# When the weight copies of a seven-product stage are stored, and how fast its weight sums are formed: a sliding-window attention and mixer kernel on one core

## The chip, the cores and the metric

The kernel runs on one core of one Trainium2 chip. The metric is device time in microseconds (us) of one execution; lower is better. The kernel before takes 866.21 us, the median of three runs (866.21, 866.83 and 866.21). One further execution was profiled: it took 867.31 us, and its span from the first to the last instruction is 865.5 us.

The core has five instruction queues that run side by side and meet only through semaphores: TensorE (PE, whose weight loads are listed apart as PEld), VectorE (DVE), ScalarE (ACT), GpSimd (POOL) and SyncE (SP). In this kernel SP issues nearly all DMA transfers, in the order of its queue. Each queue is worked through in order: an instruction that waits holds up all that stand behind it on its engine.

## The reference, cut to what matters

Eight batches of 576 tokens, eight heads of 64. Attention looks back over a window of 64 positions; its result, laid out as `x` with 576 rows of 512 per batch, goes through a token mixer and a channel mixer.

```python
scores = where((rel >= 0) & (rel < 64), q @ k.T / 8, -1e9)
x = softmax(scores) @ v                                   # per batch: 576 x 512
h = maximum(x.T @ w_tok1, 0) @ w_tok2                     # 512 x 576, over the tokens
u = x + h.T
h2 = maximum(u @ w_ch1, 0) @ w_ch2                        # 512 -> 1536 -> 512
out = u + h2
```

The four weight matrices arrive as 64-bit floats. Everything below happens in the last two lines: the channel mixer with `w_ch1` (512 x 1536) and `w_ch2` (1536 x 512).

## The kernel before

**Precision.** An fp32 matrix is held as two parts, `hi` (its rounding to the type float32r) and `lo` (the rest), and a product is three matmuls: hi by hi, hi by lo, lo by hi. Writing a part pair takes one ACT instruction (`hi`, a copy or a Relu) and one DVE instruction (`lo`, a subtraction).

**The two stages.** The first stage works over 36 tiles of attention and the token mixer and leaves `u` in DRAM (`u_dram`). The second stage is the channel mixer. It takes the 8 * 576 = 4608 tokens in nine chunks of 512. For one chunk, the *first product* makes twelve row blocks (`ft` = 0 to 11, 128 of the 1536 hidden rows each): `gemm1` is 12 matmuls (4 blocks of the 512 input rows times 3) into one PSUM bank `gp`, then `relu_split` writes `ghi` on ACT (line 607) and `glo` on DVE (line 608). The *second product* makes four output blocks (`ct` = 0 to 3): `gemm2` runs over the hidden blocks into a bank `op`, `add_out` adds the bank to `uf` on DVE (line 633) and, when the output block is complete, SP stores it (line 635).

**Chunks 0 to 2 are plain.** Chunk 0 runs all twelve `gemm1`, then four `gemm2` of 36 matmuls each. Chunks 1 and 2 run in two halves: six `gemm1` (72 matmuls), then four `gemm2` of 18 matmuls (72 matmuls), then the same for the other six blocks. In the first half of chunk 1, `load_u` fetches chunk 2's `u`; in the second half, behind `ft` = 8, `split_u` splits it into parts (four ACT and four DVE instructions).

**Chunks 3 to 8 go in pairs.** For a pair of chunks the first product is done as a 2 x 2 x 2 block product with seven products instead of eight (`PRODUCTS`: m1, m6, m7, m5, m2, m4, m3; line 839). Its weights are seven combinations of four quarters of `w_ch1`. Three of them (m1, m2, m4) are quarters as they are; four (m5, m7, m6, m3) are sums and differences. All seven, in both parts, must lie in DRAM (`w1s`) in the order in which they will be read: from chunk 2 on, `load_w1` reads them back in pieces, over the place in SBUF that held the plain weights `w1hi` and `w1lo`.

**Who makes `w1s`.** The generator `weight_steps` does it during chunk 1. Its first call issues twelve stores from SP, 384 KB each: m1, m2 and m4, two column blocks each, two parts each, straight from `w1hi` and `w1lo`. Then follow sixteen steps, four for each of n = 0 to 3 (a quarter of the work: 384 columns of one column block). With n fixed, the four steps are:

- A: two DVE additions (hi + lo) make `wa` and `ws`.
- B: two DVE additions, then `keep("m5")`.
- C: two DVE subtractions, then `keep("m7")` and `keep("m6")`.
- D: one DVE addition, one DVE subtraction, then `keep("m3")`.

A `keep` is a split (one ACT cast `whi`, one DVE subtraction `wlo`) and two stores of 192 KB from SP. The tiles `whi` and `wlo` have four buffers each, so a `keep` must wait until the two stores of the `keep` four before it have landed.

**What sets the order.** The order of each engine's queue is the order in which the code is written; there is no scheduler. In chunk 1 each `gemm1` with its `relu_split` is followed by two calls of the generator (lines 768 to 770). The generator's instructions so stand in the ACT and DVE queues between one block's `ghi` and `glo` and the next block's.

Of the kernel before, what the change touches and what calls it, by code (L numbers as in the profile page):

```python
# [10 lines left out]
F32 = mybir.dt.float32  # L11
# [11 lines left out]
P = 128  # L23
# [7 lines left out]
NCT = C // P  # L31
# [52 lines left out]
def mixer_kernel(ctx: ExitStack, tc: tile.TileContext, qh, kh, vh, wt1, wt2, wc1, wc2, out):  # L84
# [464 lines left out]
    with ExitStack() as bctx:  # L549
# [91 lines left out]
            return ps.tile([P, CHUNK], F32, name=f"op{name}_{ct}", tag=tag, bufs=bufs)  # L641


        u = ul.pop(0)
        for ft in range(NFT):
            gemm1(0, ft, u, gbuf[ft])
# [10 lines left out]
        for ct in range(NCT):  # L657
            for _ in range(7):
                next(late, None)
            assert all(n in finished for n in range(23 + 4 * ct, 27 + 4 * ct))  # L660
            op = new_op("0", ct)
            gemm2(op, ct, range(NFT), gbuf, True, True)
            add_out(0, u[0], ct, op, True)
        tctx.close()


        pw = tctx.enter_context(tc.tile_pool(name="pw", bufs=1, reuse_waits="tile"))

        def store_w1(m, k, f0, ct, src):

            nf = src.shape[1] // P
            nc.sync.dma_start(w1s[k][:, f0:f0 + nf, PRODUCTS.index(m), ct],  # L672
                              src.bitcast(F32).rearrange("p (f c) -> p f c", c=P))

        def weight_steps():
            for m, half, ct0 in (("m1", 0, 0), ("m2", 0, 2), ("m4", 1, 2)):
                for ct in range(2):
                    for k, w in enumerate((w1hi, w1lo)):
                        o = (half * NCT + ct0 + ct) * NH * P
                        store_w1(m, k, 0, ct, w[:, o:o + NH * P])  # L680
            yield
            nf = CW // P
            for n in range(2 * NH // nf):
                ct, f0 = n % 2, n // 2 * nf

                def whole(tag, half, ct):
                    o = (half * NCT + ct) * NH * P + f0 * P
                    t = pw.tile([P, CW], F32, name=f"{tag}_{n}", tag=tag, bufs=1)
                    nc.vector.tensor_add(t, w1hi[:, o:o + CW].bitcast(F32), w1lo[:, o:o + CW].bitcast(F32))
                    return t  # L690

                def keep(m, x):
                    hi, lo = (pw.tile([P, CW], F32R, name=f"w{k}_{m}_{n}", tag=f"w{k}", bufs=4) for k in ("hi", "lo"))
                    split(nc.scalar, nc.vector, hi, lo, x)
                    for k, t in enumerate((hi, lo)):
                        store_w1(m, k, f0, ct, t)

                a = whole("wa", 1, ct)
                s1 = whole("ws", 1, 2 + ct)
                yield  # L700
                nc.vector.tensor_add(s1, s1, a)
                c = whole("wb", 0, ct)
                keep("m5", s1)
                yield
                nc.vector.tensor_sub(a, c, a)
                nc.vector.tensor_sub(c, s1, c)
                keep("m7", a)
                keep("m6", c)
                yield
                d = whole("wd", 0, 2 + ct)  # L710
                nc.vector.tensor_sub(d, d, c)
                keep("m3", d)
                yield
# [43 lines left out]
        for j in range(1, N_PLAIN):  # L757
# [5 lines left out]
            for half in range(2):  # L763
                g = []
                for ft in range(half * NH, (half + 1) * NH):
                    g.append(new_g(f"{j}_{ft}"))
                    gemm1(j, ft, u, g[-1])
                    if j == 1:
                        for _ in range(2):
                            next(steps, None)  # L770
                    if not last and ft == 3:
                        ul[j + 1] = load_u(j + 1, pu)
                    if not last and ft == 8:
# [25 lines left out]
                for ct in range(NCT):  # L799
                    op = new_op(f"{j}_{half}", ct)  # L800
                    gemm2(op, ct, range(half * NH, (half + 1) * NH), g, True, True)
                    add_out(j, u[0], ct, op, half == 1)
                    if last and half == 1 and ct == 1:
                        sums(False)
                        sum4()
# [134 lines left out]
```

## Time and profile before

| | us |
|---|---|
| median of three runs | 866.21 |
| the profiled execution | 867.31 |
| its span | 865.5 |
| PE busy in the span | 828.6 (96%) |
| DVE busy | 527.3 (61%) |
| ACT busy | 336.4 (39%) |

The kernel is one pass over PE with little idle time: the chain of work that ended last lies on PE for 77% of the span. The stage of the seven products is the largest piece of it (line 839, 18% of that chain). Such a profile is read from PE: where PE waits or runs slowly, the question is which queue it waits for, and what that queue was waiting for in turn. In the trace, chunk 0's second product ends at 350.73 us, chunk 1 runs from there to about 427 us, and chunk 2 follows.

Two columns need a word. In the timeline rows, a matmul's duration (0.39 us for 128 x 512) is longer than the step from one start to the next (0.23 us), because matmuls are pipelined; the pace is read from the starts. `PEclk` is the share of full speed that the clock of TensorE was granted.

### The profile page before, as it was taken

The numbers are of one execution on the slowest core, as the hardware profiler recorded it, in microseconds if no ns is written. First come the engines' busy times: TensorE is split into PE (matmuls) and PEld (weight loads), VectorE is DVE, ScalarE is ACT, GpSimd is POOL, SyncE is SP. The second block draws the span as 40 slices with busy tenths as digits, with TensorE's granted clock in tenths as the row PEclk, the third lists the DMA queues.
The fourth block names the chain that finished last, engine by engine and source line by source line (L and its number), as shares of the span: only waits on it lengthen the run. The fifth ranks groups of instructions, "written<-read, shape, count | busy, mean of one in ns | idle before, by whom it ended". The sixth has DMA issues, their size and how long they took to land.

```text
span 865.5 us, 14815 instructions
## 1 busy us (share of the span) xinstructions
PE 828.6 (96%) x5864; PEld 680.8 (79%) x5864; DVE 527.3 (61%) x939; ACT 336.4 (39%) x1018; POOL 104.8 (12%) x109
## 2 busy tenths in 40 slices
PE   6889999989989999969999999999999999999998
PEld 4668878868879878848888888887888888888886
DVE  4989878878885598555244443447735367635252
ACT  4778778778786351122022120213211123202020
POOL 3533343333332000000000000000000000000000
PEclk9999999999999999979999999999999999999999
DMA  9657676666644542792240751606361424542002
GB/s 323 201 189 250 191 247 220 217 210 232 207 153 132 161 141 85 204 275 82 87 154 1 267 200 69 219 1 218 109 256 60 159 86 135 182 182 86 1 0 98
DMA packets 71334, 136.11 MB, mean 157 GB/s; under 512 B 7008, under 2 KB 41568, under 8 KB 69344
## 3 DMA queue, kind: packets, MB, share of 16 engines
q1 hardware_dynamic: 69152, 133.32, 45.9%
q10 hardware_dynamic: 2112, 1.84, 0.6%
q8 instruction: 46, 0.75, 0.4%
q14 instruction: 24, 0.20, 0.1%
HBM read 104.46 MB, written 30.67 MB: 156 GB/s over the span
## 4 chain that ended last, share of the span: by engine, by line
PE 77%; DVE 10%; ACT 4%; SPq 2%; issue 2%; POOL 2%; DMA 2%; POOLq 0%; DVEq 0%; ACTq 0%
PE gp L839 18%; PE op L628 11%; PE gp L620 6%; PE h L368 5%; PE up L410 4%; PE s L276 4%; PE op_4a L628 4%; PE op_2b L628 4%; PE op_2a L628 4%; PE op_0b L628 4%; PE op_0a L628 4%; PE op_4b L628 4%; PE xp L323 3%; PE up L403 2%; SPq L672 2%
## 5 line engine op out<-in xcount | busy, mean ns | idle before, releaser
L839 PE MATMUL gp<-m,w1hi 128*128 128x512 f32 x504 | 155.4, 389 | 0.7 <-DVE x L847 0.7
L839 PEld LDWEIGHTS gp<-m,w1hi 128*128 128x128 f32 x504 | 94.5, 188 | 20.9 <-DVE x L847 1.5
L839 PE MATMUL gp<-m,w1lo 128*128 128x512 f32 x252 | 98.0, 389 | 0.0
L304 ACT ACTIVATE e<-e,nm 128x128 f32<-128x128 f32 x232 | 90.4, 396 | 8.2 <-DVE nm L296 8.2
L607 ACT ACTIVATE ghi<-x 128x512 fp32r<-128x512 f32 x54 | 34.1, 632 | 119.9 <-DVE x L849 68.3
L843 ACT COPY x<-gp 128x512 f32<-128x512 f32 x18 | 10.4, 578 | 143.8 <-PE gp L839 143.8
L607 ACT ACTIVATE ghi<-gp 128x512 fp32r<-128x512 f32 x50 | 29.6, 595 | 82.7 <-PE gp L620 82.5
L608 DVE SCALAR_TENSOR_TENSOR glo<-x,ghi 128x512 fp32r<-128x512 f32 x54 | 37.4, 693 | 38.1 <-ACT ghi L607 38.1
L628 PE MATMUL op<-ghi,w2hi 128*128 128x512 f32 x128 | 51.4, 401 | 6.0 <-ACT ghi L607 6.0
L620 PE MATMUL gp<-ulo,w1hi 128*128 128x512 f32 x144 | 56.0, 389 | 0.0
L620 PE MATMUL gp<-uhi,w1hi 128*128 128x512 f32 x144 | 56.0, 389 | 0.0
L620 PE MATMUL gp<-uhi,w1lo 128*128 128x512 f32 x144 | 56.0, 389 | 0.0
L839 PEld LDWEIGHTS gp<-m,w1lo 128*128 128x128 f32 x252 | 47.3, 188 | 9.9
L628 PE MATMUL op<-glo,w2hi 128*128 128x512 f32 x128 | 51.3, 401 | 0.9 <-DVE glo L608 0.8
L628 PE MATMUL op<-ghi,w2lo 128*128 128x512 f32 x128 | 51.0, 398 | 0.0
L104 POOL TENSOR_TENSOR xlo<-x,xhi 128x512 fp32r<-128x512 f32 x32 | 42.6, 1332 | 65.2 <-ACT xhi L101 64.8
L323 PEld LDWEIGHTS xp<-v,pt 128*64 128x64 f32 x1152 | 37.4, 137 | 16.5 <-ACT pt L313 6.2
L608 DVE SCALAR_TENSOR_TENSOR glo<-gp,ghi 128x512 fp32r<-128x512 f32 x50 | 34.2, 686 | 25.8 <-ACT ghi L607 25.7
L276 PE MATMUL s<-k,q 64*64 64x128 f32 x1152 | 43.4, 287 | 3.4 <-DVE c L207 1.9
L323 PE MATMUL xp<-v,pt 128*64 128x64 f32 x1152 | 43.2, 226 | 2.6 <-ACT pt L313 2.2
L304 ACT ACTIVATION_READ_ACCUMULATOR e<-e,nm 128x1 f32 x232 | 44.7, 193 | 0.0
L313 ACT COPY pt<-pp 128x512 f32<-128x512 f32 x72 | 41.9, 586 | 6.6 <-PE pp L311 6.4
(165 smaller groups left out, 1894.6 us busy)
## 6 DMA issues: line engine op xcount, KB each, us to landing
v<-vh SPq DMA_DIRECT2D x36, 512.0 KB, 3.7
w1hi<-w1s SPq DMA_DIRECT2D x18, 896.0 KB, 4.8
w1lo<-w1s SPq DMA_DIRECT2D x18, 896.0 KB, 6.6
raw<-wc SPq DMA_DIRECT2D x32, 384.0 KB, 4.4
q<-qh SPq DMA_DIRECT2D x36, 256.0 KB, 4.5
k<-kh SPq DMA_DIRECT2D x7, 1280.0 KB, 7.6
out<-uf SPq DMA_DIRECT2D x35, 256.0 KB, 2.6
uf<-u_dram SPq DMA_DIRECT2D x8, 1024.0 KB, 8.7
```

The costliest lines, as they stand in the source:

```text
L104: eng_lo.tensor_sub(lo, src, hi.bitcast(F32))
L276: nc.tensor.matmul(s[u][half * BLK:(half + 1) * BLK, j], qt[r, j, half], kbs[b][r, j, n * BLK:n * BLK + P], start=not on_pe, stop=True, sk ...
L304: nc.scalar.activation(e[:, h], src[:, h], AF.Exp, bias=nm[:, g:g + 1], scale=by, accum_out=sm[:, g:g + 1])
L313: nc.scalar.copy(pt, pp)
L323: nc.tensor.matmul(xp[half * BLK:(half + 1) * BLK, h], pts[h % 2][:, h // 2, half * BLK:(half + 1) * BLK], vt[:, half, h], start=True, sto ...
L368: nc.tensor.matmul(h_ps[b][tt], w[:, o + tt * P:o + (tt + 1) * P], x, start=first and n == 0, stop=last and n == len(combos) - 1)
L410: nc.tensor.matmul(up[:, :n], hx[:, cs], w[:, tt * S + s0:tt * S + s0 + n], start=False, stop=(k == 6), skip_group_check=True)
L607: nc.scalar.activation(hi, src, AF.Relu)
L608: nc.vector.scalar_tensor_tensor(out=lo, in0=src, scalar=0.0, in1=hi.bitcast(F32), op0=ALU.max, op1=ALU.subtract)
L620: nc.tensor.matmul(gp, w[:, w1_at(ft, ct)], x[:, ct], start=(k == 0), stop=(k == 3 * NCT - 1))
L628: nc.tensor.matmul(op, w[:, ct, ft], x[:, cols], start=(first and k == 0), stop=(last and k == 3 * len(gs) - 1), skip_group_check=not (fir ...
L839: nc.tensor.matmul(b, w[:, at], c[:, h, t], start=(n < 4 and k == 0), stop=(k == 5), skip_group_check=True)
```

## The change

Two things move; no work is added or taken away. The twelve stores of plain quarters leave `weight_steps` and are issued in chunk 0's second product, three behind each of its four `add_out`. And `weight_steps`, now sixteen steps without the first call, is called once instead of twice behind each `gemm1` of chunk 1, and once more behind each `add_out` of chunk 1.

```diff
+        def store_w1(m, k, f0, ct, src):
+            nf = src.shape[1] // P
+            nc.sync.dma_start(w1s[k][:, f0:f0 + nf, PRODUCTS.index(m), ct],
+                              src.bitcast(F32).rearrange("p (f c) -> p f c", c=P))
+
+        quarters = [(m, k, ct, (half * NCT + ct0 + ct) * NH * P) for m, half, ct0 in
+                    (("m1", 0, 0), ("m2", 0, 2), ("m4", 1, 2)) for ct in range(2) for k in range(2)]
...
             op = new_op("0", ct)
             gemm2(op, ct, range(NFT), gbuf, True, True)
             add_out(0, u[0], ct, op, True)
+            for m, k, t, o in quarters[3 * ct:3 * ct + 3]:
+                store_w1(m, k, 0, t, (w1hi, w1lo)[k][:, o:o + NH * P])
         tctx.close()
...
         def weight_steps():
-            for m, half, ct0 in (("m1", 0, 0), ("m2", 0, 2), ("m4", 1, 2)):
-                for ct in range(2):
-                    for k, w in enumerate((w1hi, w1lo)):
-                        o = (half * NCT + ct0 + ct) * NH * P
-                        store_w1(m, k, 0, ct, w[:, o:o + NH * P])
-            yield
...
                     gemm1(j, ft, u, g[-1])
                     if j == 1:
-                        for _ in range(2):
-                            next(steps, None)
+                        next(steps, None)
...
                     add_out(j, u[0], ct, op, half == 1)
+                    if j == 1:
+                        next(steps, None)
```

The queue of PE is the same instruction for instruction. What moves stands on SP, ACT and DVE. In the rows below a name carries the chunk or product, the block and a running number: `ghi1_4` is `ghi` of chunk 1, block 4; `whi_m5_1` is the hi part of m5 for n = 1; `w1s0` and `w1s1` are the two parts of the array in DRAM.

SP, at the end of chunk 0 and the start of chunk 1. Before, the four stores of outputs, then the twelve quarters, then the first sums:

```order
L635 DMA out<-uf0_4246 128x512 x4
L672 DMA w1s0_69<-w1hi_66 768x1x128
L672 DMA w1s1_70<-w1lo_67 768x1x128
...
L672 DMA w1s0_69<-w1hi_66 768x1x128
L672 DMA w1s1_70<-w1lo_67 768x1x128
L672 DMA w1s0_69<-whi_m5_0_5010 128x3x128
L672 DMA w1s1_70<-wlo_m5_0_5011 128x3x128
```

Now:

```order
L635 DMA out<-uf0_4246 128x512
L647 DMA w1s0_69<-w1hi_66 768x1x128
L647 DMA w1s1_70<-w1lo_67 768x1x128
L647 DMA w1s0_69<-w1hi_66 768x1x128
L635 DMA out<-uf0_4246 128x512
...
L635 DMA out<-uf0_4246 128x512
L647 DMA w1s1_70<-w1lo_67 768x1x128
L647 DMA w1s0_69<-w1hi_66 768x1x128
L647 DMA w1s1_70<-w1lo_67 768x1x128
L647 DMA w1s0_69<-whi_m5_0_5010 128x3x128
```

Nine of the twelve stores now stand ahead of the last output store of chunk 0, and three behind it; the stores of the sums follow those three. Further down the same queue the load of chunk 2's `u` now stands behind the stores of n = 0; before it stood behind six of the eight of n = 1.

ACT, first half of chunk 1, from block 3 to block 5. Before:

```order
L607 ACTIVATE ghi1_3_5060<-gp1_3_5062 128x512
L101 CAST whi_m5_1_5080<-ws_1_5058 128x384
L101 CAST whi_m7_1_5088<-wa_1_5056 128x384
L101 CAST whi_m6_1_5094<-wb_1_5078 128x384
L607 ACTIVATE ghi1_4_5104<-gp1_4_5106 128x512
L101 CAST whi_m3_1_5124<-wd_1_5121 128x384
L607 ACTIVATE ghi1_5_5134<-gp1_5_5136 128x512
```

Now:

```order
L607 ACTIVATE ghi1_3_5047<-gp1_3_5049 128x512
L101 CAST whi_m3_0_5067<-wd_0_5064 128x384
L607 ACTIVATE ghi1_4_5077<-gp1_4_5079 128x512
L607 ACTIVATE ghi1_5_5098<-gp1_5_5100 128x512
L101 CAST whi_m5_1_5118<-ws_1_5096 128x384
```

The casts of n = 1 stood ahead of blocks 4 and 5; now the first of them stands behind block 5.

DVE, second half of chunk 1, from block 8 to block 11. Before, the last step is done at block 8 and only `split_u` and the blocks' own work follow:

```order
L608 SCALAR_TENSOR_TENSOR glo1_8_5325<-gp1_8_5326,ghi1_8_5324 128x512
L689 TENSOR_TENSOR wd_3_5341<-w1hi_66,w1lo_67 128x384
L711 TENSOR_TENSOR wd_3_5341<-wd_3_5341,wb_3_5302 128x384
L104 TENSOR_TENSOR wlo_m3_3_5345<-wd_3_5341,whi_m3_3_5344 128x384
L104 TENSOR_TENSOR ulo2_5102<-uf2_5100,uhi2_5101 128x512 x4
L608 SCALAR_TENSOR_TENSOR glo1_9_5359<-gp1_9_5360,ghi1_9_5358 128x512
L608 SCALAR_TENSOR_TENSOR glo1_10_5376<-gp1_10_5377,ghi1_10_5375 128x512
L608 SCALAR_TENSOR_TENSOR glo1_11_5393<-gp1_11_5394,ghi1_11_5392 128x512
```

Now the four steps of n = 3 lie between them:

```order
L104 TENSOR_TENSOR ulo2_5075<-uf2_5073,uhi2_5074 128x512 x4
L608 SCALAR_TENSOR_TENSOR glo1_9_5327<-gp1_9_5328,ghi1_9_5326 128x512
L701 TENSOR_TENSOR ws_3_5316<-ws_3_5316,wa_3_5314 128x384
L689 TENSOR_TENSOR wb_3_5344<-w1hi_66,w1lo_67 128x384
L104 TENSOR_TENSOR wlo_m5_3_5347<-ws_3_5316,whi_m5_3_5346 128x384
L608 SCALAR_TENSOR_TENSOR glo1_10_5353<-gp1_10_5354,ghi1_10_5352 128x512
L705 TENSOR_TENSOR wa_3_5314<-wb_3_5344,wa_3_5314 128x384
L706 TENSOR_TENSOR wb_3_5344<-ws_3_5316,wb_3_5344 128x384
L104 TENSOR_TENSOR wlo_m7_3_5372<-wa_3_5314,whi_m7_3_5371 128x384
L104 TENSOR_TENSOR wlo_m6_3_5378<-wb_3_5344,whi_m6_3_5377 128x384
L608 SCALAR_TENSOR_TENSOR glo1_11_5384<-gp1_11_5385,ghi1_11_5383 128x512
```

Seven instructions that stood ahead of `glo` of block 9 now stand between it and `glo` of block 11; the two additions of step A stay ahead of `split_u`.

More of the change, by code (lines that the diff above doesn't have):

```diff
@@ L663, in mixer_kernel @@
             add_out(0, u[0], ct, op, True)
+            for m, k, t, o in quarters[3 * ct:3 * ct + 3]:
+                store_w1(m, k, 0, t, (w1hi, w1lo)[k][:, o:o + NH * P])
         tctx.close()
         pw = tctx.enter_context(tc.tile_pool(name="pw", bufs=1, reuse_waits="tile"))
[L669 to L673, printed above, removed]
         def weight_steps():
-            for m, half, ct0 in (("m1", 0, 0), ("m2", 0, 2), ("m4", 1, 2)):
-                for ct in range(2):
-                    for k, w in enumerate((w1hi, w1lo)):
-                        o = (half * NCT + ct0 + ct) * NH * P
-                        store_w1(m, k, 0, ct, w[:, o:o + NH * P])
-            yield
             nf = CW // P
```

## The prediction

> **What bounds the kernel now.** First the page, for the engine that carries the time:
>
> ```profile
> span 865.5 us, 14815 instructions
> PE 828.6 (96%) x5864; PEld 680.8 (79%) x5864; DVE 527.3 (61%) x939; ACT 336.4 (39%) x1018; POOL 104.8 (12%) x109
> PEclk9999999999999999979999999999999999999999
> ```
>
> PE is busy 96% of the span, so only two things can be gained: PE's idle time, and stretches in which its clock is low. The clock row has one low slice, the 18th from the left (a slice is 21.6 us, so 368 to 389 us). Next the second stage cut at the borders of chunk 1's four parts (columns: length, busy us of PE, PEld, DVE, ACT, POOL with instructions, clock, DMA share, GB/s):
>
> ```profile
> 334.50:350.70 16.20, 16.20 (x73) 13.43 (x72) 7.96 (x18) 1.48 (x3) 0.00 (x0) 1.00 0.13 50
> 350.70:367.00 16.30, 16.30 (x73) 13.51 (x72) 11.31 (x21) 4.24 (x8) 0.00 (x0) 1.00 0.89 256
> 367.00:394.80 27.80, 20.86 (x73) 15.45 (x73) 12.04 (x22) 4.57 (x9) 0.00 (x0) 0.82 0.80 223
> 394.80:411.10 16.30, 16.30 (x73) 13.52 (x72) 11.85 (x22) 6.26 (x13) 0.00 (x0) 1.00 0.39 109
> 411.10:427.40 16.30, 16.30 (x73) 13.51 (x72) 4.83 (x8) 1.46 (x3) 0.00 (x0) 1.00 0.17 61
> ```
>
> Four parts of the same 72 matmuls: three take 16.3 us, the second product of the first half takes 27.8 at a clock of 0.82. PE's own timeline shows how (start, duration, instruction, idle before it and its releaser):
>
> ```profile
> 350.73 0.39 PE L620 MATMUL gp<-uhi,w1hi 128*128 128x512 f32 x1
> ...
> 369.54 0.39 PE L628 MATMUL op<-ghi,w2lo 128*128 128x512 f32 x1
> 375.05 0.79 PE L628 MATMUL op<-ghi,w2hi 128*128 128x512 f32 x1 [5.13 <-ACT ghi L607]
> ...
> 378.04 0.80 PE L628 MATMUL op<-ghi,w2hi 128*128 128x512 f32 x1 [0.92 <-ACT ghi L607]
> 379.67 0.79 PE L628 MATMUL op<-glo,w2hi 128*128 128x512 f32 x1 [0.84 <-DVE glo L608]
> ...
> 384.53 0.44 PE L628 MATMUL op<-ghi,w2hi 128*128 128x512 f32 x1
> ...
> 394.81 0.39 PE L620 MATMUL gp<-uhi,w1hi 128*128 128x512 f32 x1
> ```
>
> PE waits 5.13 us for `ghi` of block 4, then 0.92 and 0.84 us for block 5; until 384.53 it also runs slowly. Why was `ghi` late? ACT's timeline:
>
> ```profile
> 363.75 0.59 ACT L607 ACTIVATE ghi<-gp 128x512 fp32r<-128x512 f32 x1
> 371.25 0.51 ACT L101 CAST whi_m<-ws 128x384 fp32r<-128x384 f32 x1 [6.90 <-DMA w1s<-whi_m]
> ...
> 374.41 0.59 ACT L607 ACTIVATE ghi<-gp 128x512 fp32r<-128x512 f32 x1
> ...
> 377.39 0.59 ACT L607 ACTIVATE ghi<-gp 128x512 fp32r<-128x512 f32 x1
> ```
>
> The cast of m5 for n = 1 stands ahead of block 4's `ghi` and waits 6.90 us for a buffer, that is, for the store of m5 for n = 0 to land. SP's timeline and the landing times say why that store was late:
>
> ```profile
> 351.64 0.33 SPq L635 DMA_DIRECT2D out<-uf  x1
> 352.02 0.52 SPq L672 DMA_DIRECT2D w1s<-w1hi  x1
> 352.58 0.70 SPq L672 DMA_DIRECT2D w1s<-w1lo  x1
> 353.32 0.87 SPq L672 DMA_DIRECT2D w1s<-w1hi  x1
> ...
> 365.28 1.34 SPq L672 DMA_DIRECT2D w1s<-w1lo  x1
> 366.72 1.27 SPq L672 DMA_DIRECT2D w1s<-whi_m  x1
> DMA to landing us min/median/max: 2.1/3.3/7.8
> ```
>
> The twelve quarters occupy SP from 352.02 to 366.62, each 1.34 us once the queues are full; the cast they hold up ran at 358.30. It is this queue of stores, not the arithmetic, that stops ACT and through it PE.
>
> **The change part by part.** *What the stall costs.* The first half of chunk 1 takes 394.81 - 350.73 = 44.08 us. Without a wait and at full clock it is two runs of 72 matmuls, whose price stands in the chain of waits for the undisturbed second half:
>
> ```profile
> 394.97 16.32 PE gp L620 x72
> 411.29 16.32 PE op L628 x72
> ```
>
> 2 * 16.32 = 32.64 us, so 44.08 - 32.64 = 11.44 us are lost. Of these 5.13 + 0.92 + 0.84 = 6.89 are waits; the other 4.55 are matmuls at half clock (and steps between them). This is the whole of what can be gained here. Behind 400 us PE's waits are these two (total, times, longest), so nothing else is on offer there:
>
> ```profile
> PE gp L839 <- DVE x L847: 0.7, 2, 0.3
> PE op_4b L628 <- DVE uf L633: 0.5, 1, 0.5
> ```
>
> *The twelve stores, moved.* They go into chunk 0's second product, where the DMA engines are busy 13% of the time (the row 334.50:350.70). The first three stand behind the first output store, which SP issued at 334.57, the next behind that of 341.54:
>
> ```profile
> 334.57 0.34 SPq L635 DMA_DIRECT2D out<-uf  x1
> 341.54 2.28 SPq L635 DMA_DIRECT2D out<-uf  x2
> ```
>
> Into empty queues three stores cost SP 0.52 + 0.70 + 0.87 = 2.09 us; into full ones 3 * 1.34 = 4.02. The third output store (before 343.82) can so be late by up to 4 us; behind it are only the next stores, and nobody reads an output. All loads of raw weights stand ahead of the first output store in the same queue. I take 0 for PE there; cover gone, the price is bounded by what the same traffic does to the same matmuls in 350.70:367.00: at a DMA share of 0.89 PE still did 72 matmuls in 16.3 us, so 0 as well. The last three follow the output store of 351.64 and are issued by 352.0 + 2.1 = 354.1, or 356.0 at worst. The first cast of a sum ran at 358.30, so the first sum's store finds SP free, about 8 us before the 366.72 of before.
>
> *The sums, one step per block.* The costs by DVE's groups in the first half:
>
> ```profile
> L608 DVE SCALAR_TENSOR_TENSOR glo<-gp,ghi 128x512 fp32r<-128x512 f32 x6 | 4.1, 687 | 3.8 <-ACT ghi L607 3.8
> L689 DVE TENSOR_TENSOR wa<-w1hi,w1lo 128x384 f32<-128x384 f32 x3 | 1.6, 549 | 0.0
> ```
>
> At 0.55 us an instruction (its other forms of 128x384 are within 0.01 of it), steps A to D are 2, 3, 4 and 3 instructions: 1.10, 1.65, 2.20, 1.65, mean 1.65. A block of the first product takes PE 16.32 / 6 = 2.72 us. Before, DVE had two steps and a `glo` there: 2 * 1.65 + 0.69 = 3.99 us, more than PE's pace; now 1.65 + 0.69 = 2.34, less. So this part removes a second cause that lay behind the first: even with free stores DVE would have fallen behind by 1.3 us a block. In the second products a block takes 4.08 us and holds one step and one `add_out` (0.69). First half: the last `ghi` and `glo` now stand ahead of every cast of n = 1, so they come 0.6 and 1.3 us after their bank is full (367.05); PE reads them as 16th and 17th of 18 matmuls, 3.4 us after. Nothing to wait for.
>
> *The tightest place* is the tail: blocks 8 to 11 now share DVE with steps A, B and C of n = 3 and with `split_u`. I lay it over the second half of before, whose PE times would be the same, all less 11.44. Step times are those that this half showed, start to start:
>
> ```profile
> 404.40 0.55 DVE L705 TENSOR_TENSOR wa<-wb,wa 128x384 f32<-128x384 f32 x1
> ...
> 406.67 0.69 DVE L608 SCALAR_TENSOR_TENSOR glo<-gp,ghi 128x512 fp32r<-128x512 f32 x1
> ...
> 409.56 2.50 DVE L104 TENSOR_TENSOR ulo<-uf,uhi 128x512 fp32r<-128x512 f32 x4
> ```
>
> Step C is 2.27. Block 8's bank fills at 402.97; `glo` about 404.9 behind step D of n = 2; step A 405.8; the four `ulo` 408.3; `glo` of 9 at 408.9; step B 1.65, 410.6; `glo` of 10 at 411.2; step C 413.5. `ghi` of 11 waits on ACT for step C's second cast and ends near 413.6, `glo` of 11 at 414.2. PE needs them at 411.13 + 15 * 0.227 = 414.5 and at 414.8. Slack 0.5 to 0.9 us. I take 0; the other end is a slip by twice the slack, a wait of about 1 us. What is late next there is step D of n = 3, stored near 416; the places in SBUF that it frees are wanted by the first loads of raw blocks, far later:
>
> ```profile
> 428.76 11.71 SPq L732 DMA_DIRECT2D r<-u_dram  x7
> ```
>
> *What a small wait costs.* In the stall, 6.89 us of waits cost 11.44, a factor of 1.66. Against that stands one short wait:
>
> ```profile
> 318.00:324.00 6.00, 4.26 (x20) 3.22 (x19) 5.79 (x13) 2.76 (x6) 0.00 (x0) 1.00 0.33 73
> ```
>
> 1.74 us idle, and the clock stayed 1.00. By this row a wait of 1 us costs 1.0, by the stall's factor 1.7; I take the first for the estimate, the second for the range. (The Trainium skill, "TensorE: Matmul & The Clock Gate", Part 1, states that the clock falls to half after an idle window of about 3.4 us and returns after a busy one of that length. Both rows fit it: 5.13 us lost the clock, 1.74 did not; the return took 9.5 us, with two more waits inside. By it a slip at the tail would cost itself alone.)
>
> *The sum,* against the profiled execution: 867.31 (span 865.5, 1.81 around it) - 11.44 + 0 = 855.87. The median of the runs is 1.10 lower than that execution, so the forecast for a median is 866.21 - 11.44 = **854.8 us**.
>
> **The rivals.** *A short wait at the tail (or behind block 5).* DVE's pace leaves 0.5 us. If casts and subtractions wait on each other a little more than laid out, PE waits 0.3 to 2.3 us at `ghi` or `glo` of block 11. For it: seven DVE instructions put between blocks 9 and 11; against it: no step was slower than taken. At 1.4 us, 854.8 + 1.4 = 856.2; at 2.3 with the factor, 858.6.
>
> *Only the queue's length counted, and stores stay slow.* If stores land at the 7.8 us of the crowded stretch also when spread, the m5 cast of n = 1 (now near 369) still finds its store landed (issued near 359, landed by 367). So half the gain would need another cause, such as a wait of about 3 us that loses the clock: 3 * 1.66 = 5, so 860.
>
> *The same stall, moved to the second half, dearer.* m5 of n = 3 (needed near 409.4 on the old scale) waits for the store of m5 of n = 2, now issued near 397.5 behind everything else on SP. It decides when that store lands later than 12 us after issue. Then ACT is held ahead of `ghi` of 10 and 11 as it was ahead of 4 and 5, for 11.44 us, with 2.50 us of `ulo` now inside the stretch: 13.94 - 11.44 = 2.5 slower, 868.7. Against it: 7.8 is the longest landing seen, at a DMA share of 0.89 and more; the second half, with its own stores of sums, ran at 0.39.
>
> *It doesn't do what it says:* the last three quarters cannot leave before the output store of 351.64. They are three, not twelve; the rows of the order show it. I give it no time of its own.
>
> **How the numbers follow.** Stall gone: 0.70, 854.8. Short wait: 0.20, 856.2. Half the gain: 0.06, 860. Stall moved: 0.04, 868.7. The likeliest gives the time. The range holds the first two and the scatter of the runs (0.6): 853.8 to 858.2; what lies above is the last two cases and some of the second's end. A change below 0.2% (1.7 us) cannot be told from none by these runs. Faster by more: the first three, 0.96. The last case, 0.04, is slower (0.03) or comes out even (0.01).
>
> **What would show it.** Right: the second product of chunk 1's first half takes 16.3 us at clock 1.00; no slice of the clock row is low; ACT's cast of m5 waits for no DMA; quarters are issued from 334.9 on, the first sum before 360. DMA share near 0.3 or more in 334 to 351. Tail: no wait of PE near 401 to 404 (the old 412 to 415). Wrong: PE waits for `ghi` (line 607 there too) above 3 us, or DVE waits for a landing, or the gain is seen but given back behind chunk 1, where the loads of `w1s` would then come late.

## The result, and the profile after

The kernel with the change takes 855.79 us (median of four runs, 855.03 to 856.29). The kernel before, run beside it on the same chip, takes 866.52. The ratio is 0.9869, with an interval of 0.985 to 0.9889: about 10.7 us are gained. The profiled execution after took 855.03 us, 12.28 less than that of before.

First the page of the kernel after, the three lines that answer to those of before:

```profile
span 853.2 us, 14815 instructions
PE 824.0 (97%) x5864; PEld 678.7 (80%) x5864; DVE 526.1 (62%) x939; ACT 336.8 (39%) x1018; POOL 105.3 (12%) x109
PEclk9999999999999999999999999999999999999999
```

The low slice in the clock row is gone. PE's busy time fell by 4.6 us, though its instructions are the same: matmuls at half clock count as longer busy time. Next the windows of the kernel after: the second half of chunk 0's second product, then chunk 1's four parts (columns as in the prediction: length, busy us of PE, PEld, DVE, ACT, POOL with instructions, clock, DMA share, GB/s):

```profile
333.70:349.90 16.20, 16.20 (x74) 13.39 (x73) 7.92 (x18) 1.44 (x3) 0.00 (x0) 1.00 0.82 243
349.90:366.20 16.30, 16.30 (x74) 13.49 (x72) 11.10 (x20) 4.85 (x9) 0.00 (x0) 1.00 0.71 208
366.20:382.50 16.30, 16.30 (x73) 13.51 (x72) 8.91 (x16) 2.66 (x5) 0.00 (x0) 1.00 0.55 164
382.50:398.80 16.30, 16.30 (x73) 13.51 (x72) 14.01 (x26) 7.22 (x14) 0.00 (x0) 1.00 0.36 104
398.80:415.10 16.30, 16.30 (x73) 13.49 (x73) 6.25 (x11) 2.04 (x4) 0.00 (x0) 1.00 0.44 139
```

All four parts of chunk 1 now take 16.3 us. The second product of the first half went from 27.76 to 16.32 us, which is 11.44 of the 12.28 us. The other 0.84 lies ahead of chunk 1, which starts at 349.88 and no longer at 350.73. Nearly all of it is there at chunk 0's first matmul already (282.56 against 283.38), ahead of anything that the change moves. In the profiles of the kernels below, chunk 1 starts between 349.7 and 352.9. The quarters lifted the DMA share in the first of these windows from 0.13 to 0.82, and PE's 72 matmuls there kept their pace. PE's waits behind 318 us (total, times, longest):

```profile
PE op L628 <- DVE w2lo L104: 1.7, 1, 1.7
PE gp L840 <- DVE x L848: 0.7, 2, 0.3
PE op_4b L628 <- DVE uf L633: 0.5, 1, 0.5
```

The first is the wait at 324 us that the prediction used as its row for a short wait. The other two are those of before. None lies in chunk 1. SP's timeline of the kernel after shows the quarters at their new place, and the line on landing times below it belongs to the stores of line 647 (before, line 672):

```profile
333.73 0.34 SPq L635 DMA_DIRECT2D out<-uf  x1
334.12 0.52 SPq L647 DMA_DIRECT2D w1s<-w1hi  x1
...
352.47 0.87 SPq L647 DMA_DIRECT2D w1s<-w1lo  x1
357.99 0.39 SPq L647 DMA_DIRECT2D w1s<-whi_m  x1
```

```profile
DMA to landing us min/median/max: 2.1/2.3/5.0
```

The last quarter is issued by 353.3 and the first sum at 357.99. Before, that sum had to wait for the queue until 366.72. Last, ACT of the kernel after:

```profile
366.40 0.60 ACT L607 ACTIVATE ghi<-gp 128x512 fp32r<-128x512 f32 x1 [1.91 <-PE gp L620]
368.26 0.52 ACT L101 CAST whi_m<-ws 128x384 fp32r<-128x384 f32 x1 [1.27 <-DVE ws L701]
...
376.39 0.51 ACT L101 CAST whi_m<-wd 128x384 fp32r<-128x384 f32 x1 [3.56 <-DMA w1s<-wlo_m]
...
400.27 0.59 ACT L607 ACTIVATE ghi<-gp 128x512 fp32r<-128x512 f32 x1
```

Block 5's `ghi` waits for PE, as it should. The cast of m5 for n = 1 waits for DVE's sum and not for a store. The cast of m3 for n = 1 does end its wait with the landing of a store, by the third row, but it holds up nothing that PE needs: the next `ghi` follows only at 385.44. The fourth row is block 11's `ghi`, the tightest place: it ends at 400.86, and PE needs it at 398.84 + 15 * 0.227 = 402.24.

So much for what happened. It does not yet say which of the two moves did it.

### The profile page after: what moved, and what is told of

The parts are those of the page before. It is cut to its first block, busy times and chain, and to the rows that moved or that the text cites. A ratio compares the mean times of both kernels' runs of the same rounds, so it can differ in the third digit from the quotient of the medians.

```text
span 853.2 us, 14815 instructions
## 1 busy us (share of the span) xinstructions
PE 824.0 (97%) x5864; PEld 678.7 (80%) x5864; DVE 526.1 (62%) x939; ACT 336.8 (39%) x1018; POOL 105.3 (12%) x109
## 4 chain that ended last, share of the span: by engine, by line
PE 80%; DVE 9%; ACT 4%; issue 2%; POOL 2%; DMA 1%; POOLq 0%; SPq 0%; DVEq 0%; ACTq 0%
PE gp L840 18%; PE op L628 11%; PE gp L620 8%; PE h L368 5%; PE up L410 4%; PE s L276 4%; PE op_4a L628 4%; PE op_2b L628 4%; PE op_2a L628 4%; PE op_0b L628 4%; PE op_0a L628 4%; PE op_4b L628 4%; PE xp L323 3%; PE up L403 2%; POOL xlo L104 2%
## 5 line engine op out<-in xcount | busy, mean ns | idle before, releaser
L323 PEld LDWEIGHTS xp<-v,pt 128*64 128x64 f32 x1152 | 37.4, 137 | 16.3 <-ACT pt L313 6.1
```

Source lines behind the costliest of these rows:

```text
L323: nc.tensor.matmul(xp[half * BLK:(half + 1) * BLK, h], pts[h % 2][:, h // 2, half * BLK:(half + 1) * BLK], vt[:, half, h], start=True, sto ...
```

## Experiments

### Each move alone

The prediction had two causes in a row: the queue of twelve stores first, and DVE's pace (two steps a block) as a second cause behind it. The sentence to be tested is the prediction's, that the queue, not the arithmetic, stops ACT. Against it stands DVE's pace.

**Only the stores moved.** From the kernel after, two steps stay behind each first-product block:

```diff
                     if j == 1:
-                        next(steps, None)
+                        for _ in range(2):
+                            next(steps, None)
...
                     add_out(j, u[0], ct, op, half == 1)
-                    if j == 1:
-                        next(steps, None)
```

> One part alone: the twelve stores move into chunk 0's second product, the generator is still called twice behind each block of the first product in chunk 1 and not in the second products. Theory (two causes, one behind the other): no cast waits for a landing any more, but DVE needs 3.99 us a block where PE needs 2.72, so blocks 4 and 5 are still late. Taking the 5.00 and 0.56 us of DVE's landing waits out of the trace before, ghi and glo of block 4 come near 370.0 and 370.8 and those of block 5 near 372.5 and 374.1; PE wants them at 369.8, 370.0 and 371.3, 372.5. That makes waits of about 3.6 us in several pieces, clock kept: some 858.5 us, 2.5 to 4 us above the full change. Rival (the queue of stores was the only cause): the same time as the full change, 855 to 856 us, and no wait of PE in chunk 1.

Measured: 861.93 us (861.58 to 863.06), ratio to the kernel before 0.9944 (0.993 to 0.9958). That is 5 us of the gain. Its windows, first and second product of the first half:

```profile
349.80:366.10 16.30, 16.30 (x73) 13.52 (x72) 12.31 (x23) 4.66 (x9) 0.00 (x0) 1.00 0.76 220
366.10:389.40 23.30, 19.96 (x74) 15.10 (x73) 12.91 (x24) 4.58 (x9) 0.00 (x0) 0.85 0.59 174
```

Without the queue the second product still takes 23.26 us, 6.94 too many. Its waits on PE's timeline:

```profile
370.25 0.51 PE L628 MATMUL op<-ghi,w2hi 128*128 128x512 f32 x1 [1.25 <-ACT ghi L607]
370.98 0.50 PE L628 MATMUL op<-glo,w2hi 128*128 128x512 f32 x1 [0.22 <-DVE glo L608]
373.59 0.80 PE L628 MATMUL op<-ghi,w2hi 128*128 128x512 f32 x1 [1.88 <-ACT ghi L607]
```

They sum to 3.35 us; the other 3.59 are lost to the clock. The expectation had the waits nearly right (3.6 us) but took the clock as kept, so its 858.5 us came out 3.4 too low. Neither ACT nor DVE waits for a landing in chunk 1 of this kernel. What is left is DVE's pace, here two `glo` that are two blocks apart:

```profile
361.79 0.69 DVE L608 SCALAR_TENSOR_TENSOR glo<-gp,ghi 128x512 fp32r<-128x512 f32 x1
...
370.23 0.69 DVE L608 SCALAR_TENSOR_TENSOR glo<-gp,ghi 128x512 fp32r<-128x512 f32 x1
```

They stand 8.44 us apart, while PE makes two blocks in 5.44. The prediction's own numbers give most of the size. Up to block 5's `glo` DVE has ten steps and six `glo` behind block 0's bank: 2.72 + 10 * 1.65 + 6 * 0.69 = 23.4 us. PE needs that `glo` at 16.32 + 16 * 0.227 = 19.95, so it would come 3.4 us too late. In the trace it ends at 374.26, which is 24.5 us behind chunk 1's first matmul and 4.5 too late: the sum leaves out DVE's own waits for ACT's casts, 1.66 us up to there. That its 3.4 meets PE's 3.35 us of waits is in part chance, since PE was already late and slow when it asked for this `glo`.

**Only the steps spread.** From the kernel before; the twelve stores stay the generator's first call:

```diff
                     if j == 1:
-                        for _ in range(2):
-                            next(steps, None)
+                        next(steps, None)
...
                     add_out(j, u[0], ct, op, half == 1)
+                    if j == 1:
+                        next(steps, None)
```

> The other part alone: the twelve stores stay where they were, ahead of the sums at the start of chunk 1, and the generator is called once a block and once an output block. Theory (what stops PE is a cast that waits ahead of a block's ghi): SP is full until 366.6 as before and the store of m5 for n = 0 lands near 371, but the cast that needs it now stands behind the ghi of block 5, in the second product where no block follows until 383; so no wait of PE and the time of the full change, 855 to 856 us. Rival (the stores must get out of the way): the casts still wait some 5 us and PE with them at block 6 or 7, 858 to 862 us.

Measured: 855.5 us (854.83 to 856.76), ratio 0.9868 (0.9854 to 0.9881), which is the whole gain. Four views of this kernel, of the first half: the windows, SP, ACT and one row of DVE.

```profile
350.50:366.80 16.30, 16.30 (x73) 13.50 (x72) 9.64 (x17) 4.43 (x8) 0.00 (x0) 1.00 0.90 256
366.80:383.10 16.30, 16.30 (x73) 13.50 (x73) 9.44 (x18) 3.07 (x6) 0.00 (x0) 1.00 1.01 290
```

```profile
352.39 0.69 SPq L672 DMA_DIRECT2D w1s<-w1lo  x1
...
365.09 1.34 SPq L672 DMA_DIRECT2D w1s<-w1lo  x1
366.53 1.26 SPq L672 DMA_DIRECT2D w1s<-whi_m  x1
```

```profile
367.28 0.59 ACT L607 ACTIVATE ghi<-gp 128x512 fp32r<-128x512 f32 x1
372.37 0.51 ACT L101 CAST whi_m<-ws 128x384 fp32r<-128x384 f32 x1 [4.50 <-DVE ws L701]
```

```profile
373.24 0.56 DVE L104 TENSOR_TENSOR wlo_m<-ws,whi_m 128x384 fp32r<-128x384 f32 x1 [0.48 <-DMA w1s<-wlo_m]
```

The queue is as full as before: the first sum's store is issued at 366.53, and the DMA share is 0.90 and 1.01. But the cast of m5 for n = 1 now stands behind block 5's `ghi` and not ahead of block 4's. It comes so late, at 372.37, that its row shows a wait for DVE's sum and none for a landing; only the subtraction behind it waits 0.48 us for one. What waits there holds nothing up. Moving the stores is so neither needed nor enough; spreading the steps is enough.

**The quarters last.** From the kernel before: the queue is taken out of the first half in another way, and the two steps a block stay.

```diff
         def weight_steps():
-            for m, half, ct0 in (("m1", 0, 0), ("m2", 0, 2), ("m4", 1, 2)):
...
-            yield
             nf = CW // P
...
                 yield
+            for m, half, ct0 in (("m1", 0, 0), ("m2", 0, 2), ("m4", 1, 2)):
...
+            yield
```

> As before, two calls a block, but the twelve stores are issued by the generator's last call behind all sums, in the second half of chunk 1. Theory (the place in SP's queue is what counts): the sums' stores leave at once, no cast waits for a landing; DVE's pace of two steps a block stays, so the time is that of the stores moved alone, some 858.5 us. Rival (the load of the DMA engines in chunk 1 is what counts, wherever the stores stand): a stall of several us again, in the second half of chunk 1 or when the weights are read back in chunk 2; 862 to 867 us.

Measured: 861.66 us (861.47 to 863.34), ratio 0.9942 (0.993 to 0.9955), as with the stores moved forward, and again above the expected 858.5. Its windows: the second product of the first half, and the part in which the quarters now run.

```profile
366.60:389.10 22.50, 18.93 (x73) 14.42 (x72) 12.89 (x24) 4.58 (x9) 0.00 (x0) 0.92 0.61 180
...
405.40:421.70 16.30, 16.30 (x73) 13.51 (x72) 2.77 (x4) 0.60 (x1) 0.00 (x0) 1.00 1.00 296
```

3.57 us of waits and 2.62 of clock are left, much as in the first experiment. Two kernels that take the queue away by different means agree: that alone gains 4.5 to 5.3 of the 11.44 us. Spreading the steps alone gains all of it, so these are not shares of one sum: the two steps a block are needed for any of the loss, and the queue makes it larger. The second row also shows that full DMA engines do not slow these matmuls.

**The quarters still earlier.** From the kernel after: one quarter behind each first-product block of chunk 0, not three behind each output block.

```diff
             gemm1(0, ft, u, gbuf[ft])
+            m, k, t, o = quarters[ft]
+            store_w1(m, k, 0, t, (w1hi, w1lo)[k][:, o:o + NH * P])
...
             add_out(0, u[0], ct, op, True)
-            for m, k, t, o in quarters[3 * ct:3 * ct + 3]:
-                store_w1(m, k, 0, t, (w1hi, w1lo)[k][:, o:o + NH * P])
```

> The full change with the twelve stores one product earlier: one behind each of the twelve blocks of chunk 0's first product, among the loads of raw weights on SP. Theory (a store without a wait costs only its issue, at most 1.4 us, and the loads run three buffers ahead): the same as the full change, 855 to 856 us. Rival (the loads of raw weights are held up, and the second product of chunk 0 waits for its converted weights, where PE already waits 1.7 us): 1 to 5 us more, 857 to 861, seen as a longer wait of PE for w2lo.

Measured: 855.5 us (854.86 to 858.88), ratio 0.9874 (0.9858 to 0.989), as after. The windows of chunk 0's first product and of the second product that used to stall:

```profile
282.50:315.10 32.60, 32.60 (x146) 26.97 (x145) 24.44 (x52) 14.65 (x30) 0.00 (x0) 1.00 0.87 268
...
366.00:382.30 16.30, 16.30 (x73) 13.52 (x72) 8.92 (x16) 2.65 (x5) 0.00 (x0) 1.00 0.54 164
```

With the steps spread, the place of the quarters does not matter: three places (early, as in the change, as before) give the same time.

### Pace or order: two attempts at a separation

With the stores moved alone, one could still hold ACT's order responsible: two casts of n = 1 stand ahead of each `ghi`. The first attempt takes work off DVE and keeps the order. From the kernel with only the stores moved:

```diff
-                    nc.vector.tensor_add(t, w1hi[:, o:o + CW].bitcast(F32), w1lo[:, o:o + CW].bitcast(F32))
+                    nc.gpsimd.tensor_add(t, w1hi[:, o:o + CW].bitcast(F32), w1lo[:, o:o + CW].bitcast(F32))
```

> The stores moved alone, as in e1_move_only, but the first additions of the steps (hi + lo into wa, ws, wb, wd; line 689 before) run on POOL, which is idle there. That takes 4 of 12 instructions of a quarter of the sums, 2.2 us per two blocks, off DVE: 3.99 - 1.10 = 2.9 us a block beside PE's 2.72. Theory (after the stores, DVE's pace of two steps a block is what is left): the waits of PE in the first half of chunk 1 shrink from 3.4 us to under 1, the second product there takes 16.3 to 18 us instead of 23.3, in all 855.5 to 858. Rival (what is left is the order on ACT, ghi behind casts that wait for a chain of engines, and POOL makes the chain longer at some 1 us an addition): waits as long as in e1_move_only or longer, 861 to 866.

Measured: 861.11 us (860.31 to 862.62), ratio 0.9939 (0.9924 to 0.9954). The waits shrank from 3.35 to 2.01 us, but this tells little, since the additions did not come free. Groups of this kernel on POOL, and on DVE with the minimum, median and maximum in ns of one:

```profile
L689 POOL TENSOR_TENSOR wb<-w1hi,w1lo 128x384 f32<-128x384 f32 x3 | 4.0, 1326 | 0.0
```

```profile
L711 DVE TENSOR_TENSOR wd<-wd,wb x4: 549/1364/1373, 361.8 to 399.2; 128x384 f32<-128x384 f32 x4
```

An addition takes 1.33 us on POOL, and DVE's own subtraction, which runs beside it, 1.36 us; in the kernel with only the stores moved the same one takes 0.56, and here the one that ran with POOL at rest 0.55 (the minimum). Neither side of the expectation came true: the waits are neither under 1 us nor as long as without POOL. The attempt is inconclusive.

The second attempt lets DVE just keep up: three steps over two blocks, none in the second products. Again from the kernel with only the stores moved:

```diff
-                        for _ in range(2):
+                        for _ in range(1 + ft % 2):
```

> The stores moved alone, and three calls of the generator in two blocks of the first product instead of four (one behind an even block, two behind an odd one), none in the second products. Theory (DVE's pace is what is left once the stores are moved): 1.5 * 1.65 + 0.69 = 3.2 us a block beside 2.72, so block 5 falls behind by 6 * 0.45 = 2.7 us, inside the 3.4 us that PE leaves before it reads it: no wait, second product 16.3 us, the time of the full change, 855 to 856.5. Rival (the order on ACT, ghi behind casts that wait for a chain of engines): the casts of m7 and m6 of n = 1 still stand ahead of ghi of block 5, so a wait of 1 to 2 us remains and with it a loss of clock, 858 to 860.

Measured: 862.33 us (861.26 to 864.88), ratio 0.9946 (0.9925 to 0.9967). Its windows of most of the first half's second product, and of the second half's:

```profile
366.00:382.00 16.00, 15.76 (x68) 12.48 (x67) 8.73 (x16) 2.94 (x6) 0.00 (x0) 1.00 0.59 165
399.70:421.30 21.60, 19.05 (x73) 14.54 (x72) 8.29 (x15) 3.05 (x6) 0.00 (x0) 0.92 0.35 110
```

In the first half the only wait listed for PE is 0.23 us, and the clock is kept; the part takes 17.18 us, 0.86 too many. Two steps, with their casts, still stand ahead of every second `ghi`, and it hurts little: that speaks for the pace. But the second half, which the expectation left out, now takes 21.58 us for its second product, 2.55 of it waits. DVE has seven steps, six `glo` and `split_u` there, the latter in this row:

```profile
396.35 2.50 DVE L104 TENSOR_TENSOR ulo<-uf,uhi 128x512 fp32r<-128x512 f32 x4
...
406.15 0.69 DVE L608 SCALAR_TENSOR_TENSOR glo<-gp,ghi 128x512 fp32r<-128x512 f32 x1
```

The sum used above gives 2.72 + 7 * 1.65 + 2.50 + 6 * 0.69 = 20.9 us against PE's 19.95. In the trace that `glo` ends 23.4 us behind the half's first matmul, since the sum again leaves out DVE's waits (1.95 us here). For the second half of the kernel with the whole change the same sum is 17.6, because only five steps stand ahead of that `glo`, and the trace has 19.1. So the sum orders the kernels rightly, but it runs 1.1 to 2.5 us low.

### What one wait costs

The prediction left open what a wait of PE costs beside itself: nothing by the row that ends at 324 us, two thirds of its length by the stall. Four kernels make one wait of a chosen length where the stall was. They are the kernel after with additions ahead of block 5 whose result nobody uses; nothing is left out.

```diff
+                    if j == 1 and ft == 5:
+                        scratch = pw.tile([P, CHUNK], F32, name="scratch", tag="scratch", bufs=1)
+                        for _ in range(9):
+                            nc.vector.tensor_add(scratch, w1hi[:, :CHUNK].bitcast(F32), w1lo[:, :CHUNK].bitcast(F32))
                     gemm1(j, ft, u, g[-1])
```

Nine additions:

> The full change with nine additions on a scratch tile (0.61 us each, result unused) put into DVE's queue ahead of glo of block 5 in chunk 1. That glo must start by 369.1 to cost nothing, the additions begin at 366.07: PE should wait 366.07 + 9 * 0.61 - 369.1 = 2.5 us once. Theory (a short wait costs itself, as the 1.74 us near 320 did): clock 1.00 throughout, 2.5 us more than the full change, 857.5 to 859. Rival (any wait costs 1.66 times itself, as in the stall): 4.1 us more and a slice at lower clock, 859 to 861.

Fourteen:

> The same with fourteen additions: PE should wait 366.07 + 14 * 0.61 - 369.1 = 5.5 us once. Theory (a wait as long as the 5.13 us of the stall loses the clock): the matmuls behind it run at half clock for several us, so the cost is 5.5 plus some 3 to 4.5, 864 to 866. Rival (in the stall the clock was lost through the pieces that followed, 0.92 and 0.84): clock 1.00, cost 5.5 alone, 861 to 862.

Eight:

> As e4_wait_short with eight scratch additions instead of nine. One such addition measured 0.72 us in a row, so PE should wait 3.24 - 0.72 = 2.5 us. The 1.74 us near 320 kept the clock, 3.24 us lost it for some 3.4 us at a cost of 1.9. If a wait must reach some 3 us to lose the clock: 2.5 us more than the full change, second product 18.8 us, clock 1.00. If the limit lies below 2.5: 4.4 us more, second product 20.7 us, two to three us at clock 0.50.

Seven:

> As e8_wait_2500 with seven scratch additions: PE should wait 2.51 - 0.72 = 1.8 us, once. 2.51 us lost the clock for a further 1.9 us; the 1.74 us near 320, which came in two pieces with matmuls between, kept it. If the limit lies between: second product 18.1 us at clock 1.00, 1.8 us above the full change. If any such single wait is enough: second product 20.0 us, 3.7 us above the full change.

The medians and ratios are of all runs. The last three columns are of the one profiled execution of each, by the second product's time over 16.32 us:

| additions | median, us | ratio to before (interval) | the wait, us | lost in all | beside the wait |
|---|---|---|---|---|---|
| 7 | 858.58 | 0.99 (0.9878 to 0.9922) | 1.78 | 3.73 | 1.95 |
| 8 | 860.04 | 0.9927 (0.9904 to 0.9951) | 2.51 | 4.41 | 1.90 |
| 9 | 861.2 | 0.9915 (0.9898 to 0.9932) | 3.24 | 5.15 | 1.91 |
| 14 | 864.92 | 0.9976 (0.9963 to 0.9989) | 6.86 | 8.68 | 1.82 |

In these profiles the cost beside the wait is the same for a wait of 1.78 and of 6.86 us. It is neither nothing nor a share of the wait. The first two expectations had the waits too short (2.5 us for 3.24 and 5.5 for 6.86): the 861.2 us with nine additions lie just above the higher of their ranges, and the 864.9 with fourteen lie within theirs by luck, since the loss beside the wait came out smaller (1.8 us, not 3 to 4.5). With eight and seven additions the higher loss came out as written. PE's timeline with nine additions shows what it is:

```profile
374.40 0.50 PE L628 MATMUL op<-glo,w2hi 128*128 128x512 f32 x1 [3.24 <-DVE glo L608]
...
375.10 0.63 PE L628 MATMUL op<-ghi,w2hi 128*128 128x512 f32 x1
375.53 0.63 PE L628 MATMUL op<-glo,w2hi 128*128 128x512 f32 x1
...
378.38 0.39 PE L628 MATMUL op<-ghi,w2lo 128*128 128x512 f32 x1
```

From 375.1 to 378.1 the matmuls follow each other at 0.43 us in place of 0.23; then the clock is back. With fourteen additions, windows of 2 us inside the wait and the matmuls at its end:

```profile
372.00:374.00 2.00, 0.00 (x0) 0.00 (x0) 1.90 (x4) 0.00 (x0) 0.00 (x0) 0.86 0.00 0
374.00:376.00 2.00, 0.00 (x0) 0.00 (x0) 1.90 (x4) 0.00 (x0) 0.00 (x0) 0.50 0.00 0
```

```profile
377.02 0.80 PE L628 MATMUL op<-glo,w2hi 128*128 128x512 f32 x1 [6.86 <-DVE glo L608]
...
380.18 0.43 PE L628 MATMUL op<-ghi,w2lo 128*128 128x512 f32 x1
```

Here the clock falls to half during the wait, and the slow stretch behind it lasts 3.2 us again. So one wait brings one stretch of about 3.3 us in which the matmuls run at half clock, worth about 1.9 us with the restart, whenever the clock falls.

But not every wait does. The wait for `w2lo` near 324 us stands in every kernel so far. The kernel before, and the kernel with seven additions, at that place (PE's row, then the window of each):

```profile
323.83 0.50 PE L628 MATMUL op<-ghix,w2lo 128*128 128x512 f32 x1 [1.74 <-DVE w2lo L104]
```

```profile
324.00:328.00 4.00, 4.00 (x18) 3.29 (x19) 3.83 (x10) 0.58 (x2) 0.00 (x0) 1.00 0.23 87
```

```profile
324.34 0.50 PE L628 MATMUL op<-ghix,w2lo 128*128 128x512 f32 x1 [1.79 <-DVE w2lo L104]
```

```profile
324.00:328.00 4.00, 3.66 (x10) 2.85 (x11) 3.86 (x10) 0.68 (x2) 0.00 (x0) 0.60 0.35 98
```

1.74 us kept the clock, 1.79 us of the same wait lost it. (The expectation for seven additions says that the 1.74 us came in two pieces; the row shows one.) Twelve profiles have this wait. In ten of them it is 1.52 to 1.74 us long and the clock stayed at 1.00. Beside itself it then costs 0.3 us: chunk 0's second product takes 34.66 us with a wait of 1.72 in the kernel after, and 32.64 without one in the last experiment. In two profiles, those with seven additions and with the additions on POOL, it is 1.79 and 2.13 us long, and the clock was lost (0.60 and 0.57). At this place the length alone would part the two kinds.

It does not elsewhere. In the first stage some waits of PE recur in all thirteen profiles with the same length. One near 53 us is 1.91 to 1.95 us long; the clock fell behind it in eleven profiles and stayed at 1.00 in two (with the stores moved alone, and with three steps over two blocks). Two near 180 and 247 us are 1.71 to 1.73 us long; the clock fell in three of the 26 cases. Waits of 1.85 us near 11 us and of 1.15 us near 48 us kept the clock in all thirteen. So a wait of one and the same length loses the clock in one execution and keeps it in another, and what decides is not shown. The times fit: the profiled execution with seven additions, which lost the clock at both places, is the slowest of four (861.77 us), and the other three (857.89 to 858.89) lie about where the wait alone would put them, 867.67 * 0.9869 + 1.78 + 0.3 = 858.4 (an estimate from the kernel before beside them, the ratio of the whole change, the wait and its restart). So the last column of the table is the price in an execution that loses the clock, not in every one. Several short waits can lose it too: with the additions on POOL, PE waited 0.39, 0.31, 1.02 and 0.29 us within 4 us, and one stretch at half clock followed.

The Trainium skill, "TensorE: Matmul & The Clock Gate", in its table of rules ("Why this matters for your kernels"), asks for no idle gaps of PE above about 3 us. The rows with 1.78 and 2.51 us differ from that: in these profiles such gaps lost the clock too. Its Part 1 has the clock return after about 3.4 us of work, and the 3.3 us agree.

### The wait that is left

The wait near 324 us has a cause that can be moved: in chunk 0's first product, `split_u` for chunk 1 stands behind block 8 and gives DVE 2.5 us of work ahead of the splits that PE waits for. From the kernel after:

```diff
-            if ft == 8:
-                split_u(ul[1])
         for ct in range(NCT):
...
+            if ct == 1:
+                split_u(ul[1])
```

> The full change, and split_u of chunk 1 moved from block 8 of chunk 0's first product to behind the second output block of its second product. Its four subtractions hold DVE for 2.41 us (313.43 to 315.84 in the full change) ahead of the w2lo that PE waits for near 323; chunk 1 needs them only at 350, and DVE has 7.47 us free before that. Theory: w2lo comes 2.4 us earlier, the wait of 1.74 us goes, and with it the chance of losing the clock there: 853.5 to 854.5, PE without a wait from 315 to 415. Rival (DVE then waits elsewhere: the conversions behind it are held by their loads or by ACT, so w2lo comes no earlier; or the late split delays chunk 1): 855 to 857.

Measured: 854.42 us (853.24 to 854.92), ratio 0.9848 (0.9829 to 0.9868). Waits of PE behind 300 us, and the window of chunk 0's second product, in this kernel:

```profile
PE gp L840 <- DVE x L848: 0.7, 2, 0.3
PE op_4b L628 <- DVE uf L633: 0.5, 1, 0.5
```

```profile
315.00:347.70 32.70, 32.70 (x146) 27.09 (x145) 27.63 (x59) 9.49 (x20) 0.00 (x0) 1.00 0.55 163
```

The wait is gone, and PE runs through both products of chunk 0 and all of chunk 1 without a stop. Chunk 0's second product takes 32.64 us in place of 34.66. The median is 1.4 us below that of the change, the lowest of the kernels here. But its interval overlaps that of the change (0.985 to 0.9889), and the spans of the two profiles are alike (853.0 and 853.2), since chunk 0 began 1.8 us later in this one. So the trace shows the wait removed, and the times alone do not show the difference.

## Why the prediction was right, and where its reasons were not

**The sum.** Forecast 854.8 us, measured 855.79, inside the range. The number alone lies nearer to the second case, a short wait at the tail (856.2); it is the trace, with no wait there, that decides for the first. The term of the stall, 11.44 us, came out as written: 27.76 to 16.32. The medians differ by 10.73, 0.7 less; chunk 1's start varies by 1.4 us between the profiles that kept the clock near 324 us, and that covers it.

**The stores moved.** Right throughout. The stores were issued from 334.12 on and the first sum before 360. PE's pace at a DMA share of 0.82 was undisturbed, as the row at 0.89 had said, and stayed so at 0.87, 1.00 and 1.01.

**Steps one per block, and the tail.** Right, and a little on the safe side: block 11's `ghi` had 1.4 us to spare, its `glo` 0.9, where 0.9 and 0.5 were laid out. The tail is nonetheless where this kernel is tight; with three steps over two blocks it became the stall.

**The rivals.** The short wait at the tail did not come. "Stores stay slow" and the stall moved to the second half both needed landings of 7.8 us and more; the longest was 5.0, the median 2.3.

**The step that failed** is the sentence "It is this queue of stores, not the arithmetic, that stops ACT and through it PE." It is right for the one row it was read from, the cast that waited 6.90 us. It is wrong as an account of the 11.44 us. With the queue gone and two steps a block, 6.2 to 6.9 us stay lost. With the queue in place and the steps spread, nothing is lost. The prediction did name DVE's pace as a second cause behind the first and had its size, but weighed it as a remainder. The forecast held because the change spreads the steps as well; the stores moved alone, its first cause, gained 5 us. So the number was right for a reason that the prediction ranked second.

**The price of a short wait** was left between two rates, and neither is the rule. "By this row a wait of 1 us costs 1.0" comes near what a wait costs when it keeps the clock: itself and 0.3 us. A wait of 1.15 us in the first stage kept the clock in all thirteen profiles. But longer ones, from 1.7 us on, kept it in some executions and lost it in others, so the row that was read is one of two outcomes. The stall's factor of 1.66 is no law: single waits that lost the clock cost a fixed 1.8 to 1.95 us more, a factor of 2.1 at 1.78 us and 1.27 at 6.86. At the end of the short-wait case, 2.3 us, the factor gives 3.8 us; by the runs it would be 2.6 or 4.2 (an estimate: 2.3 and 0.3, or 2.3 and 1.9). Nor is the stall's own loss explained in full: before, and with the stores moved alone, 4.55 and 3.59 us were lost beside the waits, more than 1.9, and the matmuls behind the last wait were slow for 4.9 and 5.6 us, longer than 3.3. That several waits close together lengthen the stretch is an inference from these rows, not tested by itself.

**Still open** is whether ACT's order by itself has a price: the first half with three steps over two blocks speaks against it, the trial on POOL does not decide it.

## What to carry to other kernels

When side work is woven between a pipeline's blocks, add up per block what each engine has to do and set it against the block's time on the bound engine, up to the last instruction that engine waits for; a queue that holds up one instruction explains its row, but a change of one cause at a time shows what it is worth. An instruction that may wait for a buffer does harm only where something needed stands behind it on its engine, so putting it behind the needed work can do as much as speeding up what it waits for, and more so if the buffer has come free by its new turn. Count a short wait of TensorE as its length, a restart and a possible stretch at half clock (about 0.3 us without the stretch and 1.9 with it here), and look at the second half of a schedule whenever work is moved out of the first.

## What the runs showed of the hardware

- The traced single waits of TensorE that lost the clock in the second stage (six, of 1.78 to 6.86 us) were each followed by one stretch of 3.2 to 3.4 us in which matmuls ran at half clock, and cost 1.8 to 2.0 us beside themselves. Those that kept it (ten, of 1.52 to 1.74 us) cost 0.3 us beside themselves.
- Whether a wait of a given length loses the clock varied between executions: one of 1.91 to 1.95 us near 53 us lost it in eleven profiles of thirteen, two of 1.71 to 1.73 us near 180 and 247 us in three cases of 26, and one of 1.85 us near 11 us in none of thirteen.
- VectorE's subtraction of one 128x384 fp32 tile from another took 1.36 us beside an addition on GpSimd, and 0.56 us without. The addition took 1.33 us.
- Nine additions on VectorE into one and the same tile, 128x512, took 0.72 us each (6.50 in all), where 0.61 had been laid out from other rows of its additions.
- DMA engines at a share of 1.00 (296 GB/s) cost the matmuls beside them nothing.
